# One Strassen product moved into a PSUM bank of its own, and the block's nine steps put in another order

## The chip, the cores and the metric

The kernel runs on one core of a Trainium2 chip. The metric is the device time of one execution in microseconds; of the kernel before three executions were timed, and their median counts.

## The reference

Performer attention, then a mixture of four experts, then a second two-matrix layer. Sizes: 1152 tokens, width 512, four experts with 1024 hidden columns, a second layer with 2048.

```python
def _moe_ref(x, domain_probs, w1, w2):
    p = domain_probs / (domain_probs.sum(-1, keepdims=True) + 1e-09)
    out = np.zeros((N, D), dtype=np.float32)
    for e in range(E):
        h = np.maximum(x @ w1[e], 0.0)
        out += p[:, e:e + 1] * (h @ w2[e])
    return out.astype(np.float32)

def _moe2_ref(x, w_in, w_out):
    h = x @ w_in
    g = h * np.cos(h)
    return (g @ w_out).astype(np.float32)
```

Here x is the attention's output. w_in and w_out come as 64-bit floats.

## The kernel before, in words

**Stages.** The attention takes the first part of the run. Behind it comes a stream of six "experts" e = 0 to 5: the four of the mixture, and the second layer cut into two halves of its hidden columns (e = 4, 5). Each has a first product (hidden = x @ w1) and a second product (hidden @ w2). Every fp32 operand is split into a high and a low part, and three matmuls (high-high, high-low, low-high) make one. The 1152 tokens are three chunks of 384 columns; chunk 0, 1 and 2.

**The first product** of e = 1 to 5 (`first_product`) runs over four blocks p = 0 to 3. A block makes 2 x 128 hidden rows for all three chunks. For chunks 1 and 2 it is one Strassen step: seven products of six matmuls each (128x384, `products`, L396) in four PSUM banks a, b, c, d; three of the banks are opened a second time (`reopen=True`), so that a further product adds to what stands there. For chunk 0 there are two plain products of twelve matmuls each (`plain`, steps z[0] and z[1]). So a block has 42 + 24 = 66 matmuls. The results are combined by VectorE (DVE): five adds in a block (`add`, L439), each reading one bank and one SBUF tile; ScalarE (ACT) copies bank a out (L444, and L359 after the second opening). A bank that is opened again must first have been read: the matmuls of the second opening wait for the add that reads the first. Before, the reopened banks are a, b and c, in `three` and `four`; the orders of the steps are three, by e and p (L474 to L481).

**Banks.** All of PSUM's eight banks are one pool `ps`. Each block takes six before: a, b, c, d and one for each plain product.

**The second product** (`Second.run`) runs over nine token tiles of 128 with 24 matmuls of 512 columns each (L535). Its left operands are staged two half tiles ahead (`ahead`): for e < 4 ACT makes the high part with a ReLU (L507, `sth`), DVE the low part (L508, `stl`); for e = 4, 5 ACT L105 and DVE L107 do. The first matmul of a second product needs chunk 0's hidden values of all four blocks (with e = 3 chunk 1's, as its tiles run 3 to 8 and then 0 to 2). Results go to an accumulator by DVE (L568) or ACT.

**The order of the work** is one Python generator (`dense`): the stream advances by quanta (one `yield` each: one product of six matmuls, or half of a plain product; 11 in a block, 44 in a first product), and at each quantum all running helpers are advanced: weight loads with their splits and sums (`load_a` with L105, L107, L139; `load_v2`), the cosine gate (`settle`: ACT L342, DVE L344, POOL L347, ACT L350, DVE L352), and the **conversions** of the 64-bit weights (`convert64`), one each 9 to 10 quanta from e = 0 to the middle of e = 3. A conversion is a loop over single buffers: POOL starts a load of raw bits (L175, L181); ACT takes the absolute value (L185); DVE runs L189, L192, L197, L200, L203; then ACT L214, DVE L216, L217, and POOL writes the parts to DRAM (L220). The next L185 writes the tile that L220 reads (`f64t`), so it waits until that write has landed.

Each engine takes its instructions in the order in which the generator issued them: an instruction that waits holds all behind it on its engine.

Of the kernel before, what the change touches and what calls it, by code (L numbers as in the profile page):

```python
# [12 lines left out]
ACTF = mybir.ActivationFunctionType  # L13
# [13 lines left out]
def performer_moe_kernel(ctx, tc, q, k, v, omega, probs, w1, w2, w_in, w_out, out):  # L27
    nc = tc.nc
    B, H, S, D = q.shape
    M = omega.shape[0]  # L30
    NT, DM = out.shape
    E, _, F = w1.shape
# [10 lines left out]
    CW = TC * P  # L43
# [18 lines left out]
    def bank(name):  # L62
        return ps.tile([P, 512], F32, tag="ps", name=name)
# [17 lines left out]
    NPF = FT // 2  # L81
# [147 lines left out]
    x_t, acc, h_t, t_t = {}, {}, {}, {}  # L229
# [126 lines left out]
    def settle_later(e, c, i, p, src=None):  # L356

        if src is not None:
            nc.scalar.activation(h_t[c, i][:, p, :], src, ACTF.Copy)  # L359
        if e < E:  # L360
            final[c, i, p] = e
        else:
            line.append((c, i, p, e))
# [18 lines left out]
    def new_h(c):  # L382
        for i in range(2):
            h_t[c, i] = (hp_ if c == 0 else late["hp"]).tile([P, NPF, CW], F32, tag=f"h{c}{i}", name=f"h{c}{i}")

    def products(dst, a, ao, b, start=True, stop=True, reopen=False):


        ah, al = a
        bh, bl = b  # L390
        kn = bh.shape[1]
        n = 0
        for kk in range(kn):
            o = slice(ao + kk * P, ao + (kk + 1) * P)
            for x, y in ((ah, bh), (ah, bl), (al, bh)):
                nc.tensor.matmul(  # L396
                    dst, x[:, o], y[:, kk, :], start=start and n == 0, stop=stop and n == 3 * kn - 1,
                    skip_group_check=reopen,
                )
                n += 1  # L400

    def plain(e, c, i, p):

        g = bank(f"g1_{e}_{c}_{i}_{p}")[:, :CW]
        J = KD // 2
        for j in range(2):
            products(
                g, units["a", e, p], (i * KD + j * J) * P, [x[:, j * J : (j + 1) * J, :] for x in x_t[c]],
                j == 0, j == 1,
            )  # L410
            if j == 0:
                yield
        settled(e, c, i, p, g)
        yield
# [9 lines left out]
    def first_product(e):  # L424
        for c in range(NCH):
            new_h(c)
        J = KD // 2
        for p in range(NPF):
            a, s = units["a", e, p], units["s", e, p]
            A = {(i, j): (a, (i * KD + j * J) * P) for i in range(2) for j in range(2)}  # L430
            S = {n: (s, (n - 1) * J * P) for n in range(1, 5)}
            x1, x2 = x_t[1], x_t[2]
            b11, b21 = tuple(x[:, :J, :] for x in x1), tuple(x[:, J:, :] for x in x1)
            b22 = tuple(x[:, J:, :] for x in x2)
            ba, bb, bc, bd = (bank(f"g1_{e}_{p}{n}")[:, :CW] for n in "abcd")
            h = {(i, k): h_t[k + 1, i][:, p, :] for i in range(2) for k in range(2)}

            def add(dst, x, y):
                nc.vector.tensor_tensor(out=dst, in0=x, in1=y, op=ALU.add)  # L439

            def one():
                products(ba, *A[0, 0], b11)
                yield
                nc.scalar.activation(h[0, 0], ba, ACTF.Copy)  # L444
                products(bd, *S[2], t_t[2])
                add(h[1, 0], bd, h[0, 0])
                yield

            def two():
                products(bb, *S[1], t_t[1])  # L450
                add(h[1, 1], bb, h[1, 0])
                yield
                products(bc, *S[3], t_t[3])
                add(h[1, 1], bc, h[1, 1])
                settle_later(e, 2, 1, p)
                yield

            def three():
                products(ba, *A[0, 1], b21, False, reopen=True)
                settle_later(e, 1, 0, p, ba)  # L460
                yield
                products(bb, *S[4], b22, False, reopen=True)
                add(h[0, 1], bb, h[1, 0])
                settle_later(e, 2, 0, p)
                yield

            def four():
                products(bc, *A[1, 1], t_t[4], False, reopen=True)
                add(h[1, 0], bc, h[1, 0])
                settle_later(e, 1, 1, p)  # L470
                yield

            z = [lambda i=i: plain(e, 0, i, p) for i in range(2)]
            if e == E and p == 0:  # L474
                order = [one, two, three, four, *z]
            elif p < NPF - 1:
                order = [one, z[0], two, z[1], three, four]
            elif e == E - 1:
                order = [one, z[0], two, three, four, z[1]]
            else:  # L480
                order = [*z, one, two, three, four]  # L481
            for n, step in enumerate(order):
                if n == len(order) - 1:
                    retired.update({("a", e, p), ("s", e, p)})
                yield from step()
# [171 lines left out]
    def dense():  # L657
        under = []
        for e in range(E + 2):
            if e == E - 1:  # L660
                order = [*range(TC, NTILE), *range(TC)]
            elif e == E + 1:
                order = [*range(NTILE - 3), NTILE - 1, NTILE - 3, NTILE - 2]
            else:
                order = [*range(NTILE)]
            second = Second(e, order)
            if e == 0:
                run = second.run()
                parts = [
                    first_plain(e, 0), islice(run, 4 * TC), first_plain(e, 1), first_plain(e, 2), run  # L670
                ]
            else:
                parts = [first_product(e), second.run()]
            q = 0
            for g in parts:
                for _ in g:
                    advance(settling)
                    from_line(q)
                    second.ahead()
                    if (e, q) == (0, 44):  # L680
                        late["first"].close()
                        late["T"] = ctx.enter_context(tc.tile_pool(name="tp", bufs=1))
                    advance(under)
                    for make in starts[e].get(q, ()):
                        under.append(make())
                        next(under[-1])
                    q += 1
                    yield
# [8 lines left out]
    with tc.tile_pool(name="at1", bufs=1) as at1, tc.tile_pool(name="at2", bufs=2) as at2:  # L697
# [13 lines left out]
        one = const.tile([P, 1], F32, name="one")  # L711
# [321 lines left out]
        for s in range(NPR + 3):  # L1033
# [39 lines left out]
            if 2 <= s <= NPR + 1:  # L1073
                b, hp = pairs[s - 2]
# [73 lines left out]
```

## Time and profile before

| | us |
|---|---|
| three executions | 688.40, 689.08, 690.08 |
| median | 689.08 |
| the profiled execution, its span from first to last instruction | 687.7 |
| TensorE (PE) busy | 668.4 |
| its weight loads (PEld) | 607.0 |
| VectorE (DVE) | 515.5 |
| ScalarE (ACT) | 312.5 |
| GpSimd (POOL) | 171.3 |

The profiled execution has no other time than its span, which lies 1.4 us under the median. PEld is the loading of a matmul's left operand into TensorE; it runs ahead of the matmuls, and it is where TensorE's waits show: the idle time before a weight load is the time in which the matmul that follows could not start. The page shows the granted clock of TensorE at nine tenths or more in all of its 40 slices.

### The profile page before, as it was taken

The page shows a single profiled execution, that of the slowest core. Times are in us where ns is not written, and L with a number is a line of the kernel's source. Part 1 is how long each engine was busy: PE and PEld are TensorE (multiplying, and loading weights), DVE is VectorE, ACT ScalarE, POOL GpSimd, SP SyncE. Part 2 cuts the span into 40 slices and gives each one's busy share as a digit, 9 for nine tenths or more (in the row PEclk, how much of TensorE's full clock was granted, in tenths as well). Part 3 has the DMA queues.
Part 4 walks back from the last instruction along what each step waited for, and adds up shares of the span by engine and source line. Part 5 has one row for each costly group of instructions (what it writes and reads, how often), then busy time and mean ns, then how long its engine had stood idle before and what let it go on. Part 6 is the DMA issues. An engine that isn't in the chain of part 4 may idle for free.

```text
span 687.7 us, 10009 instructions
## 1 busy us (share of the span) xinstructions
PE 668.4 (97%) x3665; PEld 607.0 (88%) x3665; DVE 515.5 (75%) x945; ACT 312.5 (45%) x626; POOL 171.3 (25%) x220
## 2 busy tenths in 40 slices
PE   8999999999998999999999999999899999999998
PEld 7999998997798888899788999887899788998887
DVE  6998645879878878787778588897677693487762
ACT  5777762344235435144343244443454563345530
POOL 8777420210101110101100111100134330134320
PEclk9999999999999999999999999999999999999999
DMA  7654001323526532446234446310700001600011
GB/s 187 188 143 135 14 1 62 112 94 101 142 103 186 152 122 92 143 128 178 69 100 120 122 125 208 112 47 9 299 31 32 1 0 45 263 1 1 38 55 47
DMA packets 51217, 68.86 MB, mean 100 GB/s; under 512 B 15072, under 2 KB 35808, under 8 KB 51168
## 3 DMA queue, kind: packets, MB, share of 16 engines
q1 hardware_dynamic: 42576, 38.82, 18.1%
q0 software_dynamic: 8448, 29.37, 13.8%
q8 instruction: 29, 0.48, 0.3%
q14 instruction: 20, 0.16, 0.1%
q10 hardware_dynamic: 144, 0.03, 0.0%
HBM read 53.27 MB, written 14.94 MB: 99 GB/s over the span
## 4 chain that ended last, share of the span: by engine, by line
PE 68%; DVE 16%; issue 5%; DMA 5%; ACT 4%; POOL 2%; DVEq 0%; POOLq 0%; ACTq 0%
PE g L535 39%; PE g L396 12%; DVE h L439 3%; PE num L919 2%; PE kv L890 2%; DMA kv_0h<-f64t 1%; DMA kv_1h<-f64t 1%; DVE rs L139 1%; PE pj_q L813 1%; PE g_0b L396 1%; PE g_0a L396 1%; PE g_0c L396 1%; PE pj_k L813 1%; PE g_3c L396 1%; PE tq L903 1%
## 5 line engine op out<-in xcount | busy, mean ns | idle before, releaser
L507 ACT ACTIVATE sth<-h 128x512 fp32r<-128x512 f32 x72 | 44.5, 626 | 45.7 <-PE g L535 41.9
L508 DVE SCALAR_TENSOR_TENSOR stl<-h,sth 128x512 fp32r<-128x512 f32 x72 | 49.0, 687 | 21.3 <-ACT sth L507 21.2
L107 DVE TENSOR_TENSOR stl<-h,sth 128x512 fp32r<-128x512 f32 x36 | 33.6, 934 | 17.7 <-ACT sth L105 17.7
L185 ACT ACTIVATE f64t<-f64r 128x512 f32<-128x512 f32 x32 | 21.3, 665 | 53.6 <-DMA f64r<-in_moe_w_in_dram 19.3
L535 PE MATMUL g<-v_2h,sth 128*128 128x512 f32 (+1 forms) x110 | 42.7, 388 | 1.1 <-ACT sth L507 1.1
L535 PE MATMUL g<-v_2h,stl 128*128 128x512 f32 (+1 forms) x110 | 42.8, 389 | 0.5 <-DVE stl L508 0.5
L535 PE MATMUL g<-v_3h,sth 128*128 128x512 f32 (+1 forms) x110 | 42.7, 388 | 0.0
L535 PE MATMUL g<-v_0h,stl 128*128 128x512 f32 (+1 forms) x110 | 42.6, 387 | 0.0
L535 PE MATMUL g<-v_0h,sth 128*128 128x512 f32 (+1 forms) x110 | 42.6, 387 | 0.0
L535 PE MATMUL g<-v_0l,sth 128*128 128x512 f32 (+1 forms) x110 | 42.5, 386 | 0.0
L535 PE MATMUL g<-v_3h,stl 128*128 128x512 f32 (+1 forms) x110 | 42.4, 386 | 0.0
L535 PE MATMUL g<-v_1h,stl 128*128 128x512 f32 (+1 forms) x110 | 42.4, 385 | 0.0
L535 PE MATMUL g<-v_1l,sth 128*128 128x512 f32 (+1 forms) x110 | 42.4, 385 | 0.0
L535 PE MATMUL g<-v_2l,sth 128*128 128x512 f32 (+1 forms) x110 | 42.4, 385 | 0.0
L535 PE MATMUL g<-v_1h,sth 128*128 128x512 f32 (+1 forms) x110 | 42.4, 385 | 0.0
L535 PE MATMUL g<-v_3l,sth 128*128 128x512 f32 (+1 forms) x110 | 42.4, 385 | 0.0
L181 POOL DMA_DIRECT2D f64r<-in_moe_w_out_dram x16 | 8.6, 539 | 134.4 <-DVE f64b L203 55.5
L347 POOL TENSOR_TENSOR cosa<-cosa,cosr 128x384 f32<-128x384 f32 x16 | 18.4, 1153 | 81.6 <-DVE cosr L344 80.6
L337 ACT ACTIVATE h<-g 128x384 f32<-128x384 f32 x48 | 23.0, 485 | 34.3 <-PE g L396 34.3
L105 ACT ACTIVATE sth<-h 128x512 fp32r<-128x512 f32 x36 | 22.4, 623 | 17.3 <-PE g L535 12.9
L568 DVE SCALAR_TENSOR_TENSOR acc<-g,pn,acc 128x512 f32<-128x512 f32 x27 | 20.2, 748 | 13.4 <-PE g L535 13.2
L210 POOL DMA_DIRECT2D ka<-f64a x16 | 9.0, 561 | 83.4 <-DVE f64a L208 83.4
(403 smaller groups left out, 2142.7 us busy)
## 6 DMA issues: line engine op xcount, KB each, us to landing
ra<-in_moe_w_dram SPq DMA_DIRECT2D x32, 256.0 KB, 3.3
rv<-in_moe_w_dram SPq DMA_DIRECT2D x16, 512.0 KB, 3.7
f64r<-in_moe_w_in_dram POOLq DMA_DIRECT2D x16, 512.0 KB, 4.5
f64r<-in_moe_w_out_dram POOLq DMA_DIRECT2D x16, 512.0 KB, 4.4
ka<-f64a POOLq DMA_DIRECT2D x16, 256.0 KB, 2.4
ra<-ka SPq DMA_DIRECT2D x8, 512.0 KB, 5.3
kt<-in_k_dram SPq DMA_DIRECT2D x8, 256.0 KB, 2.9
qt<-in_q_dram SPq DMA_DIRECT2D x8, 256.0 KB, 3.2
```

The lines of the kernel that those rows point to most:

```text
L105: nc.scalar.activation(hi, src, ACTF.Copy)
L107: eng.tensor_tensor(out=lo, in0=src, in1=hi.bitcast(F32), op=ALU.subtract)
L185: nc.scalar.activation(t.bitcast(F32), hw.bitcast(F32), ACTF.Abs)
L337: nc.scalar.activation(dst, src, ACTF.Copy)
L347: nc.gpsimd.tensor_tensor(out=vv, in0=vv, in1=kk, op=ALU.subtract)
L396: nc.tensor.matmul(dst, x[:, o], y[:, kk, :], start=start and n == 0, stop=stop and n == 3 * kn - 1, skip_group_check=reopen,)
L439: nc.vector.tensor_tensor(out=dst, in0=x, in1=y, op=ALU.add)
L507: nc.scalar.activation(hi, src, ACTF.Relu)
L508: nc.vector.scalar_tensor_tensor(out=lo, in0=src, scalar=0.0, in1=hi.bitcast(F32), op0=ALU.max, op1=ALU.subtract)
L535: nc.tensor.matmul(g, x[:, p, :], y[:, o : o + w], start=n == 0, stop=n == 3 * FT - 1)
L568: nc.vector.scalar_tensor_tensor(out=acc[t], in0=src, scalar=p_, in1=acc[t], op0=ALU.mult, op1=ALU.add)
L813: nc.tensor.matmul(pj[:, i * 256 : (i + 1) * 256], a[:, cs], b_, start=z == 0, stop=z == 2)
```

## The change

The seven products get steps of their own (`pa`, `pd`, `pb`, `pc`, `pe`, `pa2`, `pc2`). S4*B22, which before opened bank b again, now opens a fifth bank e. The sums are formed along another path: before h[1,1] = b + h[1,0], h[1,1] = c + h[1,1] and h[0,1] = b (opened twice) + h[1,0]; now h[0,1] = b + h[1,0], h[1,1] = c + h[0,1], h[0,1] = e + h[0,1]. The count of matmuls, adds, copies and quanta is the same. The ACT copy of a is issued one quantum earlier. A block now takes seven banks of eight. The orders of the nine steps are new, by e and p. Lines behind the change are ten further down, the add is L443 and the copy L447.

```diff
@@ -432,53 +432,63 @@
             x1, x2 = x_t[1], x_t[2]
             b11, b21 = tuple(x[:, :J, :] for x in x1), tuple(x[:, J:, :] for x in x1)
             b22 = tuple(x[:, J:, :] for x in x2)
-            ba, bb, bc, bd = (bank(f"g1_{e}_{p}{n}")[:, :CW] for n in "abcd")
             h = {(i, k): h_t[k + 1, i][:, p, :] for i in range(2) for k in range(2)}
+            bk = {}
+
+            def fresh(n, *args):
+                bk[n] = bank(f"g1_{e}_{p}{n}")[:, :CW]
+                products(bk[n], *args)
 
             def add(dst, x, y):
                 nc.vector.tensor_tensor(out=dst, in0=x, in1=y, op=ALU.add)
 
-            def one():
-                products(ba, *A[0, 0], b11)
+            def pa():
+                fresh("a", *A[0, 0], b11)
+                nc.scalar.activation(h[0, 0], bk["a"], ACTF.Copy)
                 yield
-                nc.scalar.activation(h[0, 0], ba, ACTF.Copy)
-                products(bd, *S[2], t_t[2])
-                add(h[1, 0], bd, h[0, 0])
+
+            def pd():
+                fresh("d", *S[2], t_t[2])
+                add(h[1, 0], bk["d"], h[0, 0])
                 yield
 
-            def two():
-                products(bb, *S[1], t_t[1])
-                add(h[1, 1], bb, h[1, 0])
+            def pb():
+                fresh("b", *S[1], t_t[1])
+                add(h[0, 1], bk["b"], h[1, 0])
                 yield
-                products(bc, *S[3], t_t[3])
-                add(h[1, 1], bc, h[1, 1])
+
+            def pc():
+                fresh("c", *S[3], t_t[3])
+                add(h[1, 1], bk["c"], h[0, 1])
                 settle_later(e, 2, 1, p)
                 yield
 
-            def three():
-                products(ba, *A[0, 1], b21, False, reopen=True)
-                settle_later(e, 1, 0, p, ba)
-                yield
-                products(bb, *S[4], b22, False, reopen=True)
-                add(h[0, 1], bb, h[1, 0])
+            def pe():
+                fresh("e", *S[4], b22)
+                add(h[0, 1], bk["e"], h[0, 1])
                 settle_later(e, 2, 0, p)
                 yield
 
-            def four():
-                products(bc, *A[1, 1], t_t[4], False, reopen=True)
-                add(h[1, 0], bc, h[1, 0])
+            def pa2():
+                products(bk["a"], *A[0, 1], b21, False, reopen=True)
+                settle_later(e, 1, 0, p, bk["a"])
+                yield
+
+            def pc2():
+                products(bk["c"], *A[1, 1], t_t[4], False, reopen=True)
+                add(h[1, 0], bk["c"], h[1, 0])
                 settle_later(e, 1, 1, p)
                 yield
 
             z = [lambda i=i: plain(e, 0, i, p) for i in range(2)]
             if e == E and p == 0:
-                order = [one, two, three, four, *z]
-            elif p < NPF - 1:
-                order = [one, z[0], two, z[1], three, four]
+                order = [pa, pd, pb, pc, pe, pa2, pc2, *z]
+            elif p < NPF - 1 or e < E - 1:
+                order = [pa, pd, pb, pc, pe, *z, pa2, pc2]
             elif e == E - 1:
-                order = [one, z[0], two, three, four, z[1]]
+                order = [pa, pd, pb, pc, z[0], pe, pa2, pc2, z[1]]
             else:
-                order = [*z, one, two, three, four]
+                order = [pa, z[0], pd, pb, pc, z[1], pe, pa2, pc2]
             for n, step in enumerate(order):
                 if n == len(order) - 1:
                     retired.update({("a", e, p), ("s", e, p)})
```

Three places, each before and after. The first is DVE in block p = 1 of e = 1. The names: g_1_1b, c, d, e are the block's banks; h_2415 to h_2418 are h[0,0], h[1,0], h[0,1], h[1,1]; a_2l, s_2l, v_1l low parts of weights (1024 columns each); f64a, f64b, f64t the tiles of a conversion. Before:

```order
L107 TENSOR_TENSOR a_2l<-ra_2_2492,a_2h 128x1024
L107 TENSOR_TENSOR s_2l<-rs_2_2546,s_2h 128x1024
L439 TENSOR_TENSOR h_2418<-g_1_1b,h_2416 128x384
L216 TENSOR_TENSOR f64a<-f64a,f64t 128x512
L217 TENSOR_TENSOR f64b<-f64a,f64b 128x512
L107 TENSOR_TENSOR v_1l<-rv_1_2518,v_1h 128x1024
L439 TENSOR_TENSOR h_2418<-g_1_1c,h_2418 128x384
L439 TENSOR_TENSOR h_2417<-g_1_1b,h_2416 128x384
L189 TENSOR_SCALAR f64t<-f64t 128x512
L192 TENSOR_SCALAR f64a<-f64t 128x512
L439 TENSOR_TENSOR h_2416<-g_1_1c,h_2416 128x384
```

and of the change:

```order
L443 TENSOR_TENSOR h_2417<-g_1_1b,h_2416 128x384
L203 SCALAR_TENSOR_TENSOR f64b<-f64r,f64t 128x512
L107 TENSOR_TENSOR a_2l<-ra_2_2493,a_2h 128x1024
L443 TENSOR_TENSOR h_2418<-g_1_1c,h_2417 128x384
L107 TENSOR_TENSOR s_2l<-rs_2_2545,s_2h 128x1024
L443 TENSOR_TENSOR h_2417<-g_1_1e,h_2417 128x384
L216 TENSOR_TENSOR f64a<-f64a,f64t 128x512
L217 TENSOR_TENSOR f64b<-f64a,f64b 128x512
L107 TENSOR_TENSOR v_1l<-rv_1_2519,v_1h 128x1024
L189 TENSOR_SCALAR f64t<-f64t 128x512
L192 TENSOR_SCALAR f64a<-f64t 128x512
L443 TENSOR_TENSOR h_2416<-g_1_1c,h_2416 128x384
```

The add of c stood behind a_2l, s_2l, L216, L217 and v_1l, and now stands behind L203 and a_2l; the second add of c is behind L189 and L192 in both.

The second is ACT at the end of e = 1's first product (block p = 3). The names: g_1_3a is the block's bank a, g_1_0_0_3 and g_1_0_1_3 those of the two plain products, h_2413 and h_2414 chunk 0's hidden values, sth the first staged operands of the second product. Before:

```order
L337 ACTIVATE h_2413<-g_1_0_0_3_2781 128x384
L507 ACTIVATE sth<-h_2413 128x512
L337 ACTIVATE h_2414<-g_1_0_1_3_2806 128x384
L507 ACTIVATE sth<-h_2414 128x512
L444 ACTIVATE h_2415<-g_1_3a 128x384
L185 ACTIVATE f64t<-f64r 128x512
L359 ACTIVATE h_2415<-g_1_3a 128x384
```

and of the change:

```order
L105 ACTIVATE v_3h<-rv_3_2719 128x1024
L447 ACTIVATE h_2415<-g_1_3a 128x384
L214 ACTIVATE f64t<-f64a 128x512
L185 ACTIVATE f64t<-f64r 128x512
L337 ACTIVATE h_2413<-g_1_0_0_3_2829 128x384
L517 ACTIVATE sth<-h_2413 128x512
L337 ACTIVATE h_2414<-g_1_0_1_3_2853 128x384
L517 ACTIVATE sth<-h_2414 128x512
L359 ACTIVATE h_2415<-g_1_3a 128x384
```

The two copies L337 with their staging instructions, which stood ahead of the conversion's L185, now stand behind it.

The third is DVE in block p = 2 of e = 5, where no conversion runs. The names: g_5_2b to e are the banks, h_5909 and h_5925 are h[1,0], a_3l and s_3l low parts of weights, cosa, cosb, cost and cosr tiles of the gate. Before:

```order
L107 TENSOR_TENSOR a_3l<-ra_3_6096,a_3h 128x1024
L344 TENSOR_SCALAR cosr<-cost 128x384
L107 TENSOR_TENSOR s_3l<-rs_3_6151,s_3h 128x1024
L439 TENSOR_TENSOR h_5911<-g_5_2b,h_5909 128x384
L352 TENSOR_TENSOR h_5909<-h_5909,cosb 128x384
L439 TENSOR_TENSOR h_5911<-g_5_2c,h_5911 128x384
L352 TENSOR_TENSOR h_5906<-g_5_0_0_2_6171,cost 128x384
L344 TENSOR_SCALAR cosr<-cosa 128x384
L439 TENSOR_TENSOR h_5910<-g_5_2b,h_5909 128x384
L344 TENSOR_SCALAR cosr<-cosb 128x384
L439 TENSOR_TENSOR h_5909<-g_5_2c,h_5909 128x384
```

and of the change:

```order
L443 TENSOR_TENSOR h_5926<-g_5_2b,h_5925 128x384
L352 TENSOR_TENSOR h_5924<-h_5924,cosa 128x384
L344 TENSOR_SCALAR cosr<-cosb 128x384
L107 TENSOR_TENSOR a_3l<-ra_3_6112,a_3h 128x1024
L443 TENSOR_TENSOR h_5927<-g_5_2c,h_5926 128x384
L107 TENSOR_TENSOR s_3l<-rs_3_6164,s_3h 128x1024
L443 TENSOR_TENSOR h_5926<-g_5_2e,h_5926 128x384
L352 TENSOR_TENSOR h_5925<-h_5925,cosb 128x384
L344 TENSOR_SCALAR cosr<-cost 128x384
L344 TENSOR_SCALAR cosr<-cosa 128x384
L352 TENSOR_TENSOR h_5922<-g_5_0_0_2_6221,cost 128x384
L443 TENSOR_TENSOR h_5925<-g_5_2c,h_5925 128x384
```

The adds of b and c moved ahead of s_3l and of the gate's L352; the second add of c has moved behind four instructions of the gate.

## Rows read from the trace of the kernel before

**Rows 1.** Page, part 1: busy time, share and instructions of each engine; TensorE.

```profile
PE 668.4 (97%) x3665; PEld 607.0 (88%) x3665; DVE 515.5 (75%) x945; ACT 312.5 (45%) x626; POOL 171.3 (25%) x220
```

**Rows 2.** Line L396: who ended its engine's idle time (us, times), whole run.

```profile
  DVE h L439: 14.5, 16
```

**Rows 3.** Timeline, weight loads of L396: start, duration, what; in brackets idle time before.

```profile
212.00 0.19 PEld L396 LDWEIGHTS g_1c<-T4h,a_1h 128*128 128x128 f32 x1 [1.76 <-DVE h L439]
...
223.65 0.19 PEld L396 LDWEIGHTS g_2b<-xh,s_2h 128*128 128x128 f32 x1 [1.30 <-DVE h L439]
...
237.37 0.19 PEld L396 LDWEIGHTS g_3c<-T4h,a_3h 128*128 128x128 f32 x1 [1.27 <-DVE h L439]
...
333.31 0.19 PEld L396 LDWEIGHTS g_3b<-xh,s_3h 128*128 128x128 f32 x1 [2.00 <-DVE h L439]
...
520.97 0.19 PEld L396 LDWEIGHTS g_2b<-xh,s_2h 128*128 128x128 f32 x1 [0.94 <-DVE h L439]
...
535.04 0.19 PEld L396 LDWEIGHTS g_3c<-T4h,a_3h 128*128 128x128 f32 x1 [1.31 <-DVE h L439]
...
606.58 0.19 PEld L396 LDWEIGHTS g_1b<-xh,s_1h 128*128 128x128 f32 x1 [0.69 <-DVE h L439]
...
619.63 0.19 PEld L396 LDWEIGHTS g_2b<-xh,s_2h 128*128 128x128 f32 x1 [1.42 <-DVE h L439]
...
633.71 0.19 PEld L396 LDWEIGHTS g_3c<-T4h,a_3h 128*128 128x128 f32 x1 [1.31 <-DVE h L439]
```

**Rows 4.** Timeline, TensorE: starts of blocks, e=1 p=0, then e=2 p=0, p=1.

```profile
188.53 0.33 PE L396 MATMUL g_0a<-xh,a_0h 128*128 128x384 f32 x1
...
287.54 0.33 PE L396 MATMUL g_0a<-xh,a_0h 128*128 128x384 f32 x1
...
299.01 0.33 PE L396 MATMUL g_1a<-xh,a_1h 128*128 128x384 f32 x1
```

**Rows 5.** Timeline, DVE: e=1 block 1, then e=5 block 2.

```profile
210.26 1.22 DVE L107 TENSOR_TENSOR v_1l<-rv,v_1h 128x1024 fp32r<-128x1024 f32 x1
...
211.39 0.55 DVE L439 TENSOR_TENSOR h<-g_1c,h 128x384 f32<-128x384 f32 x1
...
617.89 1.22 DVE L107 TENSOR_TENSOR s_3l<-rs,s_3h 128x1024 fp32r<-128x1024 f32 x1
...
619.03 0.55 DVE L439 TENSOR_TENSOR h<-g_2b,h 128x384 f32<-128x384 f32 x1
...
620.31 0.55 DVE L439 TENSOR_TENSOR h<-g_2c,h 128x384 f32<-128x384 f32 x1
```

**Rows 6.** Timeline, POOL and ACT: the conversions' loop, e=1, last row e=3.

```profile
207.96 0.54 POOL L220 DMA_DIRECT2D kv_0h<-f64t  x1 [0.58 <-ACT f64t L214]
...
213.77 0.66 ACT L185 ACTIVATE f64t<-f64r 128x512 f32<-128x512 f32 x1 [3.66 <-DMA kv_0h<-f64t]
...
229.87 0.54 POOL L220 DMA_DIRECT2D kv_1h<-f64t  x1
...
235.26 0.67 ACT L185 ACTIVATE f64t<-f64r 128x512 f32<-128x512 f32 x1 [3.35 <-DMA kv_1h<-f64t]
...
428.31 0.67 ACT L185 ACTIVATE f64t<-f64r 128x512 f32<-128x512 f32 x1 [3.27 <-DMA kv_2h<-f64t]
```

**Rows 7.** Timeline, TensorE: first matmul of the second product, e=1 and e=3.

```profile
238.53 0.40 PE L535 MATMUL g<-v_0h,sth 128*128 128x512 f32 x1
...
431.63 0.39 PE L535 MATMUL g<-v_0h,sth 128*128 128x512 f32 x1
```

**Rows 8.** Groups by line: count, busy us, mean ns, idle before.

```profile
L507 ACT ACTIVATE sth<-h 128x512 fp32r<-128x512 f32 x72 | 44.5, 626 | 45.7 <-PE g L535 41.9
...
L508 DVE SCALAR_TENSOR_TENSOR stl<-h,sth 128x512 fp32r<-128x512 f32 x72 | 49.0, 687 | 21.3 <-ACT sth L507 21.2
...
L337 ACT ACTIVATE h<-g 128x384 f32<-128x384 f32 x48 | 23.0, 485 | 34.3 <-PE g L396 34.3
...
L189 DVE TENSOR_SCALAR f64t<-f64t 128x512 f32<-128x512 f32 x32 | 13.5, 422 | 13.3 <-ACT f64t L185 13.2
```

## The prediction

> **What bounds the kernel now.** I read the page's busy shares first: TensorE is busy for 668.4 us of 687.7, so 19 us of its time are all that an edit of the order can win, and some of them belong to the attention [rows 1]. The change removes no matmul, so the question is how much of these 19 us are waits inside the first products. The view of the one line that issues their matmuls answers: before its weight loads the engine sat idle for 14.5 us, in 16 waits, and every one was ended by the add that empties a bank [rows 2]. No other releaser stands in that view, so today no first product waits for a bank, for weights or for its token operands. The timeline then says where: nine of the sixteen make 12.0 us, and the reader should see that each stands ahead of a product that reopens b or c [rows 3]. The other seven are 0.64 us or less and make 2.5 us.
>
> **Pace and slack.** A block without a wait takes 299.01 - 287.54 = 11.47 us from its first matmul to the next block's [rows 4]. With 66 matmuls that is 0.174 us each, 1.04 us for a Strassen product, 2.09 for a plain one. Before, between the end of b and its reopening lie c, a plain product and a: 4.17 us (c likewise), and in the last block of an expert only 2.08. After, b is not reopened at all, and between c and its reopening lie e, two plain products and a: 6.25 us; in the last block of e = 3, 4, 5 one plain product less, 4.17. In the first block of e = 4 it is 2.08, as before, and no large wait stands there in the rows.
>
> **Why the adds are late.** An add takes 0.55 us; it is late because DVE's queue ahead of it is long. In block 1 of e = 1 the add of c starts at 211.39 right behind v_1l (1.22) and lets its product go at 212.00, 1.76 late [rows 3, 5]. In block 2 of e = 5, s_3l (1.22) runs from 617.89, the add of b follows at 619.03, the add of c at 620.31 [rows 5]. Without its wait of 1.42 the load of 619.63 would have come at 618.21 [rows 3]; a and a plain product earlier, at 615.1, c had ended. So that add ended 620.86 - 615.1 = 5.8 us behind its product: over the old slack of 4.17, under the new one of 6.25, even if nothing moved in the queue. And s_3l moves behind it.
>
> **The sum, expert by expert.** Matmuls, adds, copies: same number, same shapes, so nothing is added or removed there. The extra bank and the moved steps are costed below.
>
> *e = 2, 4, 5.* By laying the adds out in the new queue with the old durations, I find every reopening of c covered; in e = 2 conversions run too, but the adds come out 1.5 us or more ahead. The gain is the waits of the rows: 2.00 for e = 2; 0.94 + 1.31 = 2.25 for e = 4; 0.69 + 1.42 + 1.31 = 3.42 for e = 5 [rows 3]. Of the small waits some 1.0 us lie here too. Against it stands what is late next: the plain products come last or late now, so the first operands of the second product are staged closer to its start, and in e = 4, 5 behind the cosine gate. I charge 0.5 us for each of these two starts. Together 7.7.
>
> *e = 1.* Its first product takes 238.53 - 188.53 = 50.00 us, 4.1 over four free blocks of 45.88 [rows 4, 7]; the waits of its three rows are 4.33. But DVE is here behind the conversions, and these run at their own pace: ACT's L185 stands still until a write to DRAM has landed, 5.8 us after its issue at 207.96, and again 5.4 us after the issue at 229.87 [rows 6]. DVE's L189 cannot start before it, and the adds behind L189 with it. Before, the load behind the add of b in block 2 came at 223.65 [rows 3]; the work ahead of the add of c there is the same but for s_3l moved behind (1.22) and an add moved ahead (0.55), so it ends at 223.5 to 224.3. TensorE would reopen c at 188.53 + 3 x 11.47 - 1.04 = 221.9. So a wait of 1.7 to 2.4 stays, where two of 3.06 together stood. At the end of the product the two copies of chunk 0 and their staging now stand behind L185 on ACT. If L185 starts where it did, at 235.26 [rows 6], its 0.67, the copy's 0.49 and 0.63 for sth bring 237.05; with two adds more in the loop (1.10) it is 238.15 [rows 8]. The third matmul needs stl as well, 0.69 us behind sth [rows 8], of which 0.46 pass beside the first two: the second product starts between 237.3 and 238.4, against 238.53. I take the late end, since the adds are moved ahead into that loop: 0.2 gained.
>
> *e = 3.* The same loop at its end: L185 starts at 428.31 [rows 6], and DVE's L189, L192, the add of e, L197 and L200 stand ahead of the first stl, which with it are three at 0.42, an add, and two like L508 at 0.69 [rows 8]: 3.2 us from 428.98 give 432.2, less 0.46 is 431.7. Before, the second product started at 431.63 [rows 7]. Gain 0: whatever its block waits give back (1.4) is waited for there.
>
> *Banks.* A block holds seven of eight now. The rows of before show no wait for a bank with six [rows 2]. In the new order the closest reuse is two products (2.08 us) behind the last read's product, against an add of 0.55; I cost it at nothing, from below because a bank cannot be faster, from above with one product (1.04) in each of 20 blocks, 20.8 us, which is rival five. The Trainium skill's "Perfetto Trace Analysis", section "Optimization Strategy", speaks against the change here: the same gap repeating can mean that there isn't enough PSUM for the next tile. By that rule the sum would turn into the 20.8 us of rival five; the trace has gaps, but with a releaser that is an add on the same bank, not a missing one.
>
> Sum: 7.7 + 0.2 + 0 = 7.9 us. The profiled execution's 687.7 us becomes 679.8; the median lies 1.4 above it, so 689.08 becomes **681.2**. The bounds: at best e = 1 gains 1.2, e = 3 its 1.4, and the others 8.7 without the charge, 11.3 in all: 677.8. At worst e = 1 loses 0.7 (one more add), e = 3 loses 1.0 (sth late as well), and the others keep 5.2 (0.8 less each): 3.5 in all, 685.6.
>
> **The rivals.**
>
> One: all waits go, 689.08 - 14.5 = 674.6. For it: every wait has the same cause, and the new slack is half as long again. Against it: the landings in e = 1 and 3 [rows 6]. The Trainium skill's "Perfetto Trace Analysis", section "Optimizing Tensor Performance", Matmuls, would have it so: independent groups should rotate through different PSUM banks so that the emptying of one overlaps the next group's matmuls. Chance 0.18.
>
> Two: the waits come back at the starts of the second products. For it: both plain products end late now, and chunk 0 is what the first tiles read. If e = 2, 4 and 5 each wait for one copy, sth and stl in full (0.49 + 0.63 + 0.69 = 1.81 [rows 8]), 5.4 of the 7.9 are given back: 686.6. Against it: those experts have no landing in the way at that point. Chance 0.12.
>
> Three: the change does not do what it says: the lateness of DVE grows with the slack, since the adds form one chain (b to c to e) and c2 waits where b2 did. Then 0 to 1 us are won: 688.4. Against it: 5.8 us of lateness fit into 6.25. Chance 0.07.
>
> Four, the slower side: the conversions' loop. From 213.77 to 235.26 it makes two rounds of 10.7 us [rows 6], and they set DVE's pace in e = 1. If two adds (1.10) go into every round between L189 and L203, and TensorE pays for it in five rounds of e = 1 and of e = 3, that is 11 us against the 7.7 won elsewhere: 692.4. It decides when the last L185 of e = 1 starts over 3 us later than at 235.26. Against it: part of the round is the landing, which no add lengthens. Chance 0.04.
>
> Five: a bank is missing in each block: 681.2 + 20.8 = 702.0. Chance 0.01.
>
> **How the numbers follow.** The forecast has 0.58, with its own range of 677.8 to 685.6. The range for 8 in 10 goes from 675.5, which takes in most of rival one, to 686.8, which takes in rival two; left out are three, four, five and a third of one, 0.18. A measurement of this kernel tells 0.3%, some 2 us, from no change: faster means under 687.0. Faster: the forecast, rival one and most of two, 0.85. Within 0.3%: three and the rest of two, 0.10. Slower: four and five, 0.05.
>
> **What would show it.** Right, if the view of the matmul line shows some 4 to 6 us of waits for adds in place of 14.5, all of it ahead of c's reopening in e = 1 and 3, none of 0.5 us or more in e = 2, 4, 5; if L185 still stands before a landing for 3 us or more; and if the second products of e = 1 and 3 begin as long after their first block's start as before, within 1 us. Wrong, if first products wait for anything but adds (banks: rival five), if L535's first loads wait over 1 us in e = 2, 4, 5 (rival two), if the waits for c are as long as those for b were (rival three), or if e = 1's second product starts over 1 us later after 188.53 than now (rival four).

## The result, and the profile after

The changed kernel takes 679.13 us (median of 4 runs, 678.94 to 679.68) against 689.11 for the kernel before, timed beside it: a ratio of 0.9854 with a 95% interval of 0.984 to 0.9868, some 10.0 us less. The forecast was 7.9 us less, 681.2, and its range holds the result.

Page of the changed kernel, part 1 (before: [rows 1]):

```profile
PE 665.5 (98%) x3665; PEld 607.4 (90%) x3665; DVE 514.3 (76%) x945; ACT 312.3 (46%) x626; POOL 169.2 (25%) x220
```

TensorE has the same 3665 matmuls in a span of 677.3 us. Who ended the idle time before the weight loads of line L396, whole run (us, times; before: [rows 2]):

```profile
  DVE h L443: 1.5, 1
```

Of 14.5 us in 16 waits one wait of 1.5 is left. It has not all become time: the waits of TensorE's weight loads over the whole run, longest totals first, say what is new.

```profile
PEld g L545 <- DVE stl L518: 3.4, 7, 0.9
...
PEld g L545 <- ACT sth L517: 3.2, 3, 1.5
...
PEld tx L608 <- DVE acc L578: 1.7, 1, 1.7
...
PEld g_2c L396 <- DVE h L443: 1.5, 1, 1.5
```

Here sth and stl are the high and low parts of the staged left operands of a second product. Before, the same view had 2.3 us of waits for stl and 1.9 for sth, 2.4 less than now. What is new lies in e = 1, 2.8 us at the start of its second product and within it, where no such wait stood before, as the timeline shows (weight loads with a wait in e = 1; compare [rows 3]):

```profile
222.93 0.19 PEld L396 LDWEIGHTS g_2c<-T4h,a_2h 128*128 128x128 f32 x1 [1.52 <-DVE h L443]
...
236.88 0.19 PEld L545 LDWEIGHTS g<-v_0h,sth 128*128 128x128 f32 x1 [1.48 <-ACT sth L517]
...
237.60 0.19 PEld L545 LDWEIGHTS g<-v_0h,stl 128*128 128x128 f32 x1 [0.43 <-DVE stl L518]
...
243.51 0.19 PEld L545 LDWEIGHTS g<-v_0h,stl 128*128 128x128 f32 x1 [0.56 <-DVE stl L518]
...
279.11 0.19 PEld L545 LDWEIGHTS g<-v_2h,stl 128*128 128x128 f32 x1 [0.33 <-DVE stl L518]
```

The reader should see that the first is still an add that is late, and that the other four wait for the staged operands of the second product. The starts of the products, first matmul of each, from the timeline of TensorE (e = 1 first and second product, e = 2 and e = 3 first, e = 3 second; before: [rows 4, 7]):

```profile
188.26 0.33 PE L396 MATMUL g_0a<-xh,a_0h 128*128 128x384 f32 x1
...
236.88 0.50 PE L545 MATMUL g<-v_0h,sth 128*128 128x512 f32 x1 [1.16 <-ACT sth L517]
...
286.94 0.33 PE L396 MATMUL g_0a<-xh,a_0h 128*128 128x384 f32 x1
...
381.73 0.33 PE L396 MATMUL g_0a<-xh,a_0h 128*128 128x384 f32 x1
...
427.52 0.39 PE L545 MATMUL g<-v_0h,sth 128*128 128x512 f32 x1
```

Worked out from such starts, the length of each stretch in us:

| stretch | before | after | gain | forecast |
|---|---|---|---|---|
| to e = 1 | 188.53 | 188.26 | 0.27 | 0 |
| e = 1, first product | 50.00 | 48.62 | 1.38 | |
| e = 1, second | 49.01 | 50.06 | -1.05 | 0.2, with the line above |
| e = 2, first | 47.98 | 45.79 | 2.19 | 2.0 |
| e = 3, first | 47.11 | 45.79 | 1.32 | 0 |
| e = 4, first | 51.37 | 48.86 | 2.51 | 2.25 |
| e = 5, first | 49.64 | 45.79 | 3.85 | 3.42 |
| second products of e = 2 to 5 | 204.06 | 204.13 | -0.07 | -1.0 |
| small waits in e = 2, 4, 5 | | | in their rows | 1.0 |
| span | 687.7 | 677.3 | 10.4 | 7.9 |

A first product without a wait was put at 45.88; e = 2, 3 and 5 now take 45.79, so nothing is left to win there. (e = 4 has the transposes of its tokens in the stretch.)

### The profile page after: what moved, and what is told of

It reads as the page before. It is cut to its first block, busy times and chain, and to the rows that moved or that the text cites. A ratio compares the mean times of both kernels' runs of the same rounds, so it can differ in the third digit from the quotient of the medians.

```text
span 677.3 us, 9997 instructions
## 1 busy us (share of the span) xinstructions
PE 665.5 (98%) x3665; PEld 607.4 (90%) x3665; DVE 514.3 (76%) x945; ACT 312.3 (46%) x626; POOL 169.2 (25%) x220
## 4 chain that ended last, share of the span: by engine, by line
PE 78%; DVE 8%; issue 5%; DMA 4%; ACT 2%; POOL 2%; POOLq 0%; ACTq 0%; DVEq 0%
PE g L545 37%; PE g L396 13%; PE num L929 2%; PE kv L900 2%; PE g_0c L396 2%; DMA kv_1h<-f64t 1%; PE g_0a L396 1%; PE g_1c L396 1%; PE g_1a L396 1%; DMA f64r<-in_moe_w_in_dram 1%; PE pj_q L823 1%; PE g_3c L396 1%; PE g_3a L396 1%; PE g_2c L396 1%; PE g_2a L396 1%
## 5 line engine op out<-in xcount | busy, mean ns | idle before, releaser
L185 ACT ACTIVATE f64t<-f64r 128x512 f32<-128x512 f32 x32 | 21.3, 666 | 62.9 <-DMA f64r<-in_moe_w_in_dram 21.7
L107 DVE TENSOR_TENSOR stl<-h,sth 128x512 fp32r<-128x512 f32 x36 | 36.1, 1007 | 14.0 <-ACT sth L105 14.0
L337 ACT ACTIVATE h<-g 128x384 f32<-128x384 f32 x48 | 22.8, 485 | 33.0 <-PE g L396 32.9
```

What stands on the lines that cost most here:

```text
L107: eng.tensor_tensor(out=lo, in0=src, in1=hi.bitcast(F32), op=ALU.subtract)
L185: nc.scalar.activation(t.bitcast(F32), hw.bitcast(F32), ACTF.Abs)
L337: nc.scalar.activation(dst, src, ACTF.Copy)
```

## The experiments

The theory at the start, "slack": what counts is the time between a product and the reopening of its bank, against a DVE that comes up to 5.8 us late. Its rival, "bank": it is the fifth bank that frees the waiting product. Each run was timed beside the kernel before, whose median went from 689.53 to 690.08 us between the groups of runs, so the ratios are what to compare. Stretches and waits are those of one profiled execution of each kernel.

**1. The fifth bank in the old order.** Edit, against the changed kernel:

```diff
-            elif p < NPF - 1 or e < E - 1:
-                order = [pa, pd, pb, pc, pe, *z, pa2, pc2]
...
+            elif p < NPF - 1:
+                order = [pa, pd, z[0], pb, pc, z[1], pa2, pe, pc2]
...
-                order = [pa, z[0], pd, pb, pc, z[1], pe, pa2, pc2]
+                order = [*z, pa, pd, pb, pc, pa2, pe, pc2]
```

> The fifth bank alone: S4*B22 in its own bank, but the steps in the order of before (a, d, plain, b, c, plain, a again, e, c again). Theory 'slack': what counts is the time between c and its reopening, against a DVE that is up to 5.8 us late; it stays at 4.17 us (2.08 in the last blocks). The waits for b (7.2 of 14.5 us) go, but the add of c, half a us behind that of b, is then waited for one product later: by the rows of before some 12 of the 14.5 us stay; 687 (686 to 688). Rival 'bank': the product that was waiting gets a bank of its own, so half the waits go for good: 682 or less.

Measured: 684.91 us, 0.9933 (0.9913 to 0.9953), between the two. The waits moved one product on where that was foretold, in block 2 of e = 1 and block 3 of e = 2, where waits of 1.30 and 2.00 had stood ahead of b [rows 3] and now stand ahead of c (weight loads with their waits; the first and the last of the four stood ahead of c before, too):

```profile
211.62 0.19 PEld L396 LDWEIGHTS g_1c<-T4h,a_1h 128*128 128x128 f32 x1 [1.79 <-DVE h L443]
...
224.56 0.19 PEld L396 LDWEIGHTS g_2c<-T4h,a_2h 128*128 128x128 f32 x1 [1.54 <-DVE h L443]
...
334.24 0.19 PEld L396 LDWEIGHTS g_3c<-T4h,a_3h 128*128 128x128 f32 x1 [1.66 <-DVE h L443]
...
628.71 0.19 PEld L396 LDWEIGHTS g_3c<-T4h,a_3h 128*128 128x128 f32 x1 [1.12 <-DVE h L443]
```

But in blocks 1 and 2 of e = 4 and 5 they went altogether, though the time from c to its reopening is still 4.17 us there. Neither theory had foreseen that; experiment 3 looks for the cause.

**2. The new order with four banks.** b is opened again and the sums are formed as before, with both plain products between c and the reopenings:

```diff
             def pe():
-                fresh("e", *S[4], b22)
-                add(h[0, 1], bk["e"], h[0, 1])
+                products(bk["b"], *S[4], b22, False, reopen=True)
+                add(h[0, 1], bk["b"], h[1, 0])
...
-                order = [pa, pd, pb, pc, pe, *z, pa2, pc2]
+                order = [pa, pd, pb, pc, *z, pa2, pe, pc2]
```

> The order alone: four banks as before, b opened again, but with both plain products between c and the reopenings (a, d, b, c, plain, plain, a again, b again, c again), the same in spirit for the last blocks. From b to its reopening are then 6.25 us and from c to its reopening 6.25. Theory 'slack': 679 (678 to 680.5), the fifth bank is not needed. Rival 'bank': the waits ahead of b stay, some 4 to 7 us: 683 or more.

Measured: 677.54 us, 0.9819 (0.9803 to 0.9835), half a us under the range of "slack". The rival falls: no fifth bank is needed. First products of e = 2, 3 and 5 take 45.78 to 45.79 us, as in the changed kernel; e = 1 takes 46.81 + 49.94 against 48.62 + 50.06, and that is where it is faster (experiments 5 and 6).

**3. The copy of bank a alone.** The kernel before, with one line moved:

```diff
             def one():
                 products(ba, *A[0, 0], b11)
-                yield
                 nc.scalar.activation(h[0, 0], ba, ACTF.Copy)
+                yield
                 products(bd, *S[2], t_t[2])
```

> The kernel before, with one line moved: ACT's copy of bank a is issued before the yield, one quantum sooner, as the change does. Theory 'copy': in e=4 and 5 that copy stood on ACT behind a_3h and the gate, and DVE's add of d waited for it (5.6 us in all in the profile of before), so every later add of the block was late; with it early the waits for b in e=4 and 5 (some 3.9 us with the small ones) go: 685.5 (684.5 to 687). Rival 'bank': the 4.9 us that the fifth bank alone won came from the bank, and this line is worth nothing: 688.5 to 690.

Measured: 685.97 us, 0.9941 (0.9923 to 0.9959): faster, by 4.1 us, most of what experiment 1 won, and within the range of "copy". In the kernel before, DVE's waits name the cause (5.6 us in 4 waits: three in e = 4 and 5, one in e = 3); the second fence is ACT in block 2 of e = 5, the third DVE's add of d there:

```profile
DVE h L439 <- ACT h L444: 5.6, 4, 1.6
```

```profile
611.81 1.04 ACT L105 ACTIVATE a_3h<-ra 128x1024 fp32r<-128x1024 f32 x1
...
612.76 0.47 ACT L444 ACTIVATE h<-g_2a 128x384 f32<-128x384 f32 x1
```

```profile
613.26 0.56 DVE L439 TENSOR_TENSOR h<-g_2d,h 128x384 f32<-128x384 f32 x1 [1.59 <-ACT h L444]
```

The copy stood behind the gate and a_3h (1.04), and the add of d, with all of DVE's later work, behind it. The block had started at 609.01, so the copy ran 3.75 us after the start. With the copy issued one quantum sooner the block starts at 607.22, and ACT takes the copy 1.25 us later, ahead of a_3h:

```profile
608.47 0.49 ACT L443 ACTIVATE h<-g_2a 128x384 f32<-128x384 f32 x1
...
610.01 1.04 ACT L105 ACTIVATE a_3h<-ra 128x1024 fp32r<-128x1024 f32 x1
```

The first products of e = 4 and 5 fall from 51.37 and 49.64 us to 49.96 and 47.17, that of e = 3 from 47.11 to 46.48. Experiment 1 took 46.50, 49.95 and 46.87 in these three, so there the early copy explains what it won, but for 0.3 us in e = 5. In e = 1 the kernel with the early copy took 51.31, 1.3 more than the kernel before. There the write issued at 208.54, 0.58 later than before, let L185 go at 214.94, 6.40 us later, in place of 5.81 [rows 6].

**4. The changed kernel with the copy late again**, the same line one quantum later.

> The changed kernel, with the copy of bank a put back one quantum later. Theory 'slack': with 6.25 us between c and its reopening a DVE that is 5.8 us late still comes in time, so the order covers what the copy would cost: within 1 us of the changed kernel, 679 to 680.5. Rival 'copy': the copy carries a part of its own, and 2 to 4 us come back in e=4 and 5: 681 to 683.

Measured: 681.06 us, 0.9874 (0.9845 to 0.9903), at the border of the two and not to be told from the changed kernel's 0.9854 by this interval. By stretches the theory holds for e = 4 and 5 (48.90 and 45.79, as with the early copy), so the slack does cover it there; what was lost lies in e = 3, 46.23 + 54.05 against 45.79 + 53.14, at the reopening of c in its last block and at the second product's start (weight loads):

```profile
424.66 0.19 PEld L396 LDWEIGHTS g_3c<-T4h,a_3h 128*128 128x128 f32 x1 [0.46 <-DVE h L443]
...
429.22 0.19 PEld L545 LDWEIGHTS g<-v_0h,stl 128*128 128x128 f32 x1 [1.11 <-DVE stl L518]
```

With the copy late, e = 3 takes 100.28 us in all, as in the kernel before (100.30). The effects of copy and order do not add up: 4.1 us alone, and under the new order 1.35 in the two stretches of e = 3.

**5. The landing.** The changed kernel; for the w_out halves the absolute value goes to another tile, f64a, which in these halves no write to DRAM reads:

```diff
-        t = pool.tile([P, n], U32, tag="f64t", name="f64t")
-        nc.scalar.activation(t.bitcast(F32), hw.bitcast(F32), ACTF.Abs)
...
+        if kind == "v":
+            a = pool.tile([P, n], U32, tag="f64a", name="f64a")
+            ab = a
+        else:
+            ab = t = pool.tile([P, n], U32, tag="f64t", name="f64t")
+        nc.scalar.activation(ab.bitcast(F32), hw.bitcast(F32), ACTF.Abs)
...
```

> The changed kernel, with the conversions' absolute value (L185) written to the tile f64a instead of f64t when a w_out half is converted: L185 then no longer waits for the landing of the last write from f64t, only for the raw bits; the first write to f64t is L200, some 2 us later. Theory 'landing': the remaining waits of e=1 (1.5 us ahead of c in block 2, 1.5 at the start of its second product, some 1.0 within it) come from that landing; L185 at its end starts over 1 us sooner; 676.8 (675.5 to 678). Rival 'DVE's queue is simply full': 679, with the same waits.

Measured: 677.52 us, 0.9822 (0.9807 to 0.9836), within what was expected. e = 1 takes 46.98 + 49.84 us against 48.62 + 50.06, and the last conversion's ACT instruction there starts at 233.47 in place of 235.12; it now waits for the raw bits (line numbers are seven higher behind the edit, so L185 is L189 here):

```profile
233.47 0.67 ACT L189 ACTIVATE f64a<-f64r 128x512 f32<-128x512 f32 x1 [4.39 <-DMA f64r<-in_moe_w_out_dram]
```

The landing is what held it. At the start of the second product the wait for sth goes from 1.48 to 0.15 us; ahead of c in block 2 only from 1.52 to 1.24. In the round before that wait, DVE had stood 1.30 us for L185, which waited for the landing of the write from f64t; now DVE stands nearly as long for the landing of the conversion's other write, from f64b:

```profile
216.57 0.69 DVE L210 SCALAR_TENSOR_TENSOR f64b<-f64r,f64t 128x512 f32<-128x512 uint32 x1 [1.07 <-DMA kv_0l<-f64b]
```

The same edit in the kernel before:

> The kernel before, with the absolute value of the w_out halves written to f64a: L185 waits only for the raw bits. Theory 'landing': the waits of e=1 in the kernel before (4.3 us) hang in part on the same landing, and some 1.5 us of its 50.00 go: 687.5 (686.5 to 688.5). Rival 'slack alone': before, the adds are late by the queue, not by the landing: 689, e=1 within 0.5 us of 50.00.

Measured: 687.03 us, 0.9966 (0.9955 to 0.9978); the first product of e = 1 takes 47.86 us in place of 50.00, and every other stretch is within 0.4 of the kernel before.

**6. The place of the plain products.** The changed kernel with e behind them:

```diff
-                order = [pa, pd, pb, pc, pe, *z, pa2, pc2]
+                order = [pa, pd, pb, pc, *z, pe, pa2, pc2]
```

> The changed kernel with e after the two plain products instead of before them (a, d, b, c, plain, plain, e, a again, c again), in every block but those of e=3 to 5 with an order of their own: the positions of the four-bank kernel with the fifth bank kept. Theory 'position': what the four-bank kernel won over the changed one (some 1.5 us, in e=1) is that chunk 0's copy and staging are issued one product sooner, ahead of the conversion's L185 on ACT: 677.5 (677 to 678.3), e=1's second product starts 46.8 us after its first block. Rival 'bank': the fifth bank itself costs it: 679.

Measured: 677.83 us, 0.9823 (0.98 to 0.9845), as the four-bank kernel. By these runs the bank costs and wins nothing that can be measured; the place of the plain product does it. ACT at the end of e = 1's first product, first in the changed kernel, then here:

```profile
235.12 0.67 ACT L185 ACTIVATE f64t<-f64r 128x512 f32<-128x512 f32 x1 [5.79 <-DMA kv_1h<-f64t]
...
235.69 0.48 ACT L337 ACTIVATE h<-g 128x384 f32<-128x384 f32 x1
...
236.19 0.63 ACT L517 ACTIVATE sth<-h 128x512 fp32r<-128x512 f32 x1
```

```profile
229.88 0.49 ACT L337 ACTIVATE h<-g 128x384 f32<-128x384 f32 x1 [1.19 <-PE g L396]
...
230.41 0.64 ACT L517 ACTIVATE sth<-h 128x512 fp32r<-128x512 f32 x1
...
234.68 0.66 ACT L185 ACTIVATE f64t<-f64r 128x512 f32<-128x512 f32 x1 [3.63 <-DMA kv_1h<-f64t]
```

One product sooner, chunk 0's copy L337 and sth pass ahead of L185, and the first staged operand is there 5.8 us earlier (230.41 against 236.19). The first product takes 46.68 us, as expected; the second takes 50.53, 0.5 more than in the changed kernel, since the next operands still stand behind L185.

**7. The conversions started evenly in time.**

```diff
-        when += [(80 + (215 * i) // (n - 1), "c1") for i in range(n)]
+        at = [0.0]
+        for q in range(80, 296):
+            at.append(at[-1] + (1.04 if q >= 84 and (q - 84) % 80 < 44 else 1.36))
+        for i in range(n):
+            goal = at[215] * i / (n - 1)
+            when.append((80 + max(j for j in range(216) if at[j] <= goal + 1e-6), "c1"))
```

> The changed kernel, with the 24 later conversions started evenly in time (a quantum is 1.04 us in a first product and 1.36 in a second) instead of evenly in quanta: in a first product one each 10.5 quanta rather than 9.35. Theory 'landing': the loop no longer falls behind within e=1's first product; its waits shrink: 677 (675.5 to 678.5). Rival: the loop is late whatever its schedule, or its late rounds hit other places: 679 or more.

Measured: 678.21 us, 0.983 (0.9815 to 0.9845), inside the theory's range but nearer the rival than its middle. e = 1's first product has no wait left (45.78 us), and the second takes 51.36: the lateness moves behind the border, to stl.

```profile
241.33 0.19 PEld L545 LDWEIGHTS g<-v_0h,stl 128*128 128x128 f32 x1 [1.51 <-DVE stl L518]
...
277.51 0.19 PEld L545 LDWEIGHTS g<-v_2h,stl 128*128 128x128 f32 x1 [0.94 <-DVE stl L518]
```

**8. Order and landing together:** four banks in the new order, and the absolute value elsewhere.

> The four-bank kernel of the order-only run, with the absolute value written to f64a for the w_out halves: both edits that shorten e=1. If they take away the same wait (the landing ahead of L185) it is no faster than either: 677.5. If the second takes the waits left (1.05 us ahead of c, 1.0 within the second product): 676 (675.5 to 677).

Measured: 675.9 us, 0.9794 (0.9773 to 0.9816), the fastest of all. Both edits count: e = 1 takes 46.17 + 49.00 us, 3.5 less than in the changed kernel, and of its waits one is left (weight loads):

```profile
221.94 0.19 PEld L403 LDWEIGHTS g_2c<-T4h,a_2h 128*128 128x128 f32 x1 [0.43 <-DVE h L450]
```

**9. The changed kernel again, and the order alone.**

> The changed kernel once more, on the same chip as the two runs below, so that their differences are taken side by side: 679 (678.3 to 680), by a ratio to the kernel before of 0.985.

Measured: 680.03 us, 0.9854 (0.9836 to 0.9871), the same ratio as the first time. In this execution the wait ahead of c in e = 1 was longer:

```profile
223.72 0.19 PEld L396 LDWEIGHTS g_2c<-T4h,a_2h 128*128 128x128 f32 x1 [2.33 <-DVE h L443]
```

Here e = 1 took 49.31 + 50.22 us, 0.5 more than in the kernel before, where the first execution took 0.33 less.

Beside it the four-bank kernel of experiment 2 with the copy late as before:

> Four banks, the new order, and the copy of bank a late as before: nothing but the order is left of the change. Theory 'order': the order alone gives the most, less what the late copy cost in the changed kernel (1.3 us, at the start of e=3's second product): 678.5 to 680 against 677.5 with the early copy. Rival 'parts': without bank and copy the order gives half: 683 or more.

Measured: 679.22 us, 0.9847 (0.9831 to 0.9863). Without bank and without copy the order alone gives what the whole change gives. It is not quite the changed kernel's order: the plain products come one step sooner, which won some 2 us in experiment 6 (0.9823 against 0.9854), and the late copy costs about as much (0.9847 against experiment 2's 0.9819). In e = 4 and 5 DVE's adds of d still wait 1.41, 1.39 and 1.59 us for the copy here, and yet no first product of these waits for an add: the longer distance covers it.

## Why the prediction was right, and where it was off

The mechanism stood: fewer waits for adds, because c is reopened later; no wait for a bank; no new bound. Of its three signs of being right one came whole: L185 still stands for a landing, 5.79 us in e = 1 and 3.77 in e = 3. The view of L396 holds 1.5 us where 4 to 6 were to be left, and the second products of e = 1 and 3 begin 1.38 and 1.32 us sooner after their first block than before, where 1 was the limit: both misses are on the faster side, in e = 1 and 3. Rival three (the lateness grows with the slack) and five (a missing bank) fall by the one wait that is left in the view of L396. Rival four, the slower side, did not come: L185 at the end of e = 1 started at 235.12, against 235.26 [rows 6], where over 3 us later would have decided. Rival one, all 14.5 us, failed in e = 1, as argued, but not in e = 3, where it was argued to fail as well. (Two slips that change nothing: rival one's own 674.6 lies outside the range that is said to take in most of it, and 7.7 less three times 0.8 is 5.3, not 5.2.)

**e = 2, 4, 5: right.** 2.00, 2.25 and 3.42 were forecast from the rows, 2.19, 2.51 and 3.85 came with the small waits, 8.55 in all, where rows and small waits made 8.7. The charge of 0.5 us for each start in e = 4 and 5 was not due: second products took 0.07 and 0.05 us longer. That is 0.9 us of the 2.5 that were missed in the span; 1.3 more are e = 3.

**e = 1: right in its sum by luck, nearly right in its parts.** Forecast was a wait of 1.7 to 2.4 ahead of c in block 2, and a second product starting at 237.3 to 238.4. The wait was 1.52 (2.33 in experiment 9), the start 236.88; with the wait of 0.43 for stl, which came behind the start and not ahead of it, that is 237.31, the early end. The two adds (1.10) that made the late end were not paid: L185 started where it had. That is 1.38 won in the first product, not 0.2; but then the waits for stl within the second (0.43, 0.56 and 0.33 in the weight loads, 1.05 in its length) take most of that back, and I had priced only the first. Net 0.33 against 0.2, from two misses that cancel; in experiment 9 it was 0.5 lost.

**e = 3: the step that failed** is "Matmuls, adds, copies: same number, same shapes, so nothing is added or removed there". It put the earlier copy at nothing, and so "Gain 0: whatever its block waits give back (1.4) is waited for there" took the start of L185, 428.31 [rows 6], as fixed by the landing. It moved. ACT in e = 3, before and after:

```profile
415.16 1.06 ACT L105 ACTIVATE s_3h<-rs 128x1024 fp32r<-128x1024 f32 x1 [2.62 <-DVE rs L139]
...
416.49 0.66 ACT L185 ACTIVATE f64t<-f64r 128x512 f32<-128x512 f32 x1
```

```profile
413.21 0.68 ACT L185 ACTIVATE f64t<-f64r 128x512 f32<-128x512 f32 x1 [1.20 <-DMA kv_1h<-f64t]
...
424.06 0.66 ACT L185 ACTIVATE f64t<-f64r 128x512 f32<-128x512 f32 x1 [3.77 <-DMA kv_2h<-f64t]
```

A round earlier, in the kernel before, L185 had waited for no landing: it stood at 416.49 behind s_3h, which waited 2.62 us for DVE. So the loop was held by the queues there. The expert's first matmul came 2.79 us sooner (381.73 against 384.52), L185 4.25 us sooner, 1.46 more than TensorE. With 424.06 in place of 428.31 the prediction's own sum (0.67, 3.2, less 0.46) puts the start of the second product at 427.5; it was 427.52, and the whole 1.32 came through.

What held the queues is the late copy. In block 2 DVE's add of d waited for it, and L189, the step behind L185, stood on DVE behind that add and its followers (DVE before; then the kernel of experiment 4, which differs from the changed one in the copy alone, DVE and ACT; then DVE of the changed kernel):

```profile
412.57 0.56 DVE L439 TENSOR_TENSOR h<-g_2d,h 128x384 f32<-128x384 f32 x1 [1.23 <-ACT h L444]
...
418.52 0.42 DVE L189 TENSOR_SCALAR f64t<-f64t 128x512 f32<-128x512 f32 x1
```

```profile
409.62 0.56 DVE L443 TENSOR_TENSOR h<-g_2d,h 128x384 f32<-128x384 f32 x1 [1.23 <-ACT h L450]
...
415.76 0.42 DVE L189 TENSOR_SCALAR f64t<-f64t 128x512 f32<-128x512 f32 x1
...
425.44 0.68 ACT L185 ACTIVATE f64t<-f64r 128x512 f32<-128x512 f32 x1 [3.89 <-DMA kv_2h<-f64t]
```

```profile
414.49 0.41 DVE L189 TENSOR_SCALAR f64t<-f64t 128x512 f32<-128x512 f32 x1
```

Counted from the expert's first matmul, in us:

| kernel | copy | L189 | last L185 | both products of e = 3 |
|---|---|---|---|---|
| before | late | 34.00 | 43.79 | 100.30 |
| new order, copy late (experiment 4) | late | 34.07 | 43.75 | 100.28 |
| old order, copy early (experiment 3) | early | 32.72 | 42.56 | 99.60 |
| changed | early | 32.76 | 42.33 | 98.93 |

With the copy late the new order wins nothing in e = 3: there "Gain 0" holds. The 1.3 us came with the copy.

**The same cause elsewhere.** Experiment 3 shows the early copy worth 4.1 us by itself. The sum for e = 4 and 5 came right all the same, since the longer slack covers it (experiment 4): two remedies for one lateness. And "why the adds are late" named s_3l and v_1l, the work just ahead of the add; in e = 4 and 5 the lateness began at the add of d, with a wait of DVE for ACT.

**What of the change works.** The order. The fifth bank is not measurable: with the plain products in the same place the kernels with four and five banks are alike (0.9819 and 0.9823). The Trainium skill's "Perfetto Trace Analysis", section "Optimizing Tensor Performance", Matmuls, asks that independent groups rotate through different banks so that the emptying of one overlaps the next group's matmuls; no run here shows a gain by the extra bank that can be told from none: in the old order it won 4.9 us with the copy's 4.1 in them, 0.8 by difference and within the two intervals. The distance between a bank's first and second use did what the rotation is for. The early copy adds what e = 3 won.

**Still open:** why the landing ahead of L185 in block 1 to 2 of e = 1 differs: 5.81 us in the kernel before, 5.17 in the changed one, 5.60 in it in experiment 9, 6.40 with the copy alone. The wait ahead of c in e = 1 moves with it (1.52 at 5.17, 2.33 at 5.60); no run was made on what sets it. That it differs between two executions of one kernel says that e = 1 differs by some 0.9 us for no reason in the code.

## What to carry to other kernels

When an engine waits for the emptying of a bank, look first at how many instructions lie between its two uses, and whether independent work can be moved between them: that cost no bank here and gave 10 us (experiment 9). Follow the late instruction back along its queue to the first wait on another engine, not to the longest instruction ahead of it; here a copy issued one step sooner gave 4 us by itself. Before a loop is taken as having its own clock, check in each stretch that its landing wait is there in every round, and which queue its other steps stand in: in e = 3 a wait of 1.23 us on DVE, which the change removed, had set when the loop came round.

## What the runs showed that was not expected

Two edits that each remove the same lateness do not add: the early copy is worth 4.1 us in the old order, and in the new about 1.3 by the stretches of e = 3 (experiment 4) or 1.9 by the ratios of experiments 2 and 9. And a lateness that is pushed out of a first product can come back in the second: with the conversions spread evenly 2.8 us left the first product of e = 1 and its second became 1.3 us longer, with waits for stl.
